# Fourier mixing and hash-routed experts in one kernel: idle products first, another order in the head, and row loads issued after the relus

## The chip, the core and the metric

The kernel runs on one core of one Trainium2 chip. The metric is the device time of one execution in microseconds (us); the figure compared is the median of several runs. Engines are named as in the profile: PE (TensorE, matrix products), DVE (VectorE), ACT (ScalarE), POOL (GpSimd) and SP (SyncE, which only issues DMAs here). ACT and POOL issue DMAs too. "Clock" is the TensorE clock that the throttle granted, 1.0 being full speed.

## What is computed

```python
X = np.fft.rfft(x, axis=1)                       # x: (8, 2496, 256), f32
Y = X * (filt_r + 1j * filt_i)[None, :, :]
y = np.fft.irfft(Y, n=2496, axis=1)              # (8, 2496, 256)
t = y.reshape(19968, 256)                        # one row per token
expert_idx = token_ids * np.int64(2654435761) % np.int64(8)
for e in range(8):                               # w1: (8, 256, 1024), w2: (8, 1024, 256)
    mask = expert_idx == e
    out[mask] = np.maximum(t[mask] @ w1[e], 0.0) @ w2[e]
```

A filter over the sequence of each batch, and then a two-layer network whose weights are chosen by a hash of the token's number. All of it is f32.

## The kernel before

*The filter.* A transform of 2496 points is split into 39 by 64. Stage 1 (`stage1`, for the first two batches `stage1_c`) multiplies x with the table `wf_t` into PSUM tiles `pa`; `forward` makes the products `pb` with the table `d_t`, and DVE applies the filter; `back` makes `pc` with the table `e_t`; `stage3` multiplies with `wi_t` (`pd`), and POOL scatters the resulting token rows (L380, L382, an indirect DMA for each group of rows) to their slots in the DRAM tensor `xs`. The slots are sorted by expert, so that 256 neighbouring rows, a tile, belong to one expert. `load1`, `load2` and `load4` are the loads ahead of the three stages (x, `mid<-d` and `t<-d` in the profile); between its stages a batch goes through DRAM (`d<-mid`, written by ACT's queue), except the first two, which stay in SBUF. The products run with a ring of four PSUM tiles `fps`, which ACT and DVE empty.

*The network.* There are up to 85 tiles of 256 rows; 80 are always used, and with these inputs no more than these. For a tile i, in `step(i)`:

- `weight_sums(i + 1)`: four subtractions of 128x512 on POOL (`tw`, L792) and `store(i - 1)`: two indirect DMAs on POOL to the output;
- `up(i)`: the first layer as seven products of half size (56 matmuls, `up_a`, `up_b`, `up_c`), summed by DVE (L809); ACT copies `h21` out of PSUM (L813) after the first of them and applies four relus (L806). Between that copy and the rest stands a hook, `between`, which calls `load(i + 2)`;
- `load(i)` (L750): four DMAs of 64 KB for a tile's rows (`xg<-xs`) and one for its rows' numbers (`no<-xs`), on ACT's queue (on SP's for tiles 0 and 1);
- `weights(i + 2, 0)` and, after `down`, `weights(i + 2, 1)`: 1 MB each on SP's queue, done only if the expert changes;
- `token_parts(i + 1)` (L773) transposes the next tile's rows on DVE, `token_sums(i + 1)` makes its four sums;
- `down(i)`: 32 products `dps` (L837) with the relus' results as their weights, and a copy `osb` on DVE (L842).

*What sets the order.* Nothing is scheduled by the compiler: every engine takes its instructions as the Python code emits them. The pieces of the filter are in a list `todo` with times. Those below zero are the head (`pre`), sorted by hand-written numbers from -160 to -75: tables and x of the second batch, stage 1, the middle (`chain`), stage 3 and the scatters of the first two batches, and meanwhile the routing (`count`, `route`, `places`). Those from zero on (`main`) are in units of tiles and are emitted inside `step`: up to i + .6 after `up`, up to i + .7, .8 and .9 after each quarter of `down`, the rest after it. `begin()` opens the pools of the tiles' loop and calls `load(0)` and `load(1)`. `put_off` holds the stores of batch 2's stage 1 that are not written at once (960, 600 and 40 KB). Tiles come in five stages: those of the first stage (0 to 9) hold tokens of the first two batches only, so the loop can start when these are scattered; the later stages end at tiles 20, 30, 50 and 80.

*Shared memory.* `wts` has four slots of 1 MB: the weights of two tiles. In the head slots 0 to 2 also hold the first batch's x and later its result, and slot 3 the second's first x and then the third's.

*Counters.* In the built program the DMAs of SP and ACT together use eight completion counters in turn, in the order in which the code emits them; a DMA waits until the one eight places before it has landed.

*The end.* After the loop come, outside any condition, the transposes of tiles 80 to 84 (L773, into `mid`) and the loads of tiles 82 to 84; then nested blocks run under `tc.If(used > ...)`, none of which is taken here.

Of the kernel before, what the change touches and what calls it, by code (L numbers as in the profile page):

```python
# [11 lines left out]
F32 = mybir.dt.float32  # L12
# [7 lines left out]
P = 128  # L20
# [16 lines left out]
NU = (HN + XG) // XG  # L37
# [6 lines left out]
NT = (N + E * (TB - 1)) // TB  # L44
# [8 lines left out]
NSURE = NT - 5  # L53
# [65 lines left out]
def kernel(  # L119
# [10 lines left out]
    nc = tc.nc  # L130
# [22 lines left out]
    banks = {k: pool(ctx, f"bank_{k}", 1, PSUM) for k in "abcd"}  # L153
# [241 lines left out]
    def weights(i, which):  # L395

        if i >= NT:
            return
        if i >= 2 and which == 0:
            ws[i] = ws[i - 2][0:2]  # L400
        eng, kw = nc.scalar if i < 2 else nc.sync, {}
        if which == 0:
            ws[i].append(eng.value_load(chunk_i[0:1, 0, i:i + 1], min_val=0, max_val=E - 1))
            if i >= 2:
                ws[i].append(eng.value_load(chunk_i[0:1, 1, i:i + 1], min_val=0, max_val=1))
        e = ws[i][2]
        if i >= 2:
            kw = {"cond": ws[i][3]}
        if which == 0:


            for f in (slice(0, F // 2), slice(F // 2, F)) if i < 2 else (slice(0, F),):
                eng.dma_start(out=ws[i][0][:, :, f],
                              in_=moe_w1[bass.ds(e, 1)].rearrange("one (p dp) f -> p (one dp) f", p=P)[:, :, f], **kw)
        else:
            eng.dma_start(out=ws[i][1], in_=moe_w2[bass.ds(e, 1)].rearrange("one (fp p) d -> p (one fp) d", p=P), **kw)
# [19 lines left out]
    def load_tables(part):  # L436
        if part < 2:

            nc.gpsimd.tensor_copy(junk[:], first.x[2 * part][0:1, 0, 0:1])
        sl = S_PARTS[part]  # L440
        nc.sync.dma_start(out=d_t[:, sl, :], in_=d_dram.ap()[:, sl, :])
        for k in range(2):
            load_filter(k, sl)
# [218 lines left out]
    def spaced(t0, t1, n):  # L662
        return [t0 + (t1 - t0) * u / n for u in range(n)]
# [10 lines left out]
    def part2(b, at, loads, lag):  # L674
        bt = batches[b]
        return (within([(at[u], lambda u=u: bt.forward(u)) for u in range(NS // 2)], .3) +
                within([(at[u] + lag, lambda u=u: bt.back(u)) for u in range(NS // 2)] +
                       [(loads[g], lambda g=g: bt.load2(g)) for g in range(NS // SG)]))

    def part3(b, at, loads):  # L680
        bt = batches[b]
        return within([(at[u], lambda u=u: bt.stage3(u)) for u in range(NU)] +
                      [(loads[v], lambda v=v: bt.load4(v)) for v in range(NV)])
# [10 lines left out]
                step(batches[j // (NS // 2)], j % (NS // 2))  # L694


    todo = [(t, lambda k=k: load_tables(k)) for k, t in enumerate((-160, -159, -157, -156))]
    todo += [(t, lambda v=v: second.load1(v)) for v, t in enumerate((-158, -156.5, -156.4))]
    todo += [(t, lambda u=u: first.stage1_c(u)) for u, t in enumerate(spaced(-155, -151, NU))]
    todo += [(-154.2, count), (-152, route), (-150.9, later)]  # L700
    todo += [(-137.2, places), (-128, tile_experts), (-121, experts), (-90, blanks)]
# [2 lines left out]
    todo += [(t, lambda k=k: way_back(k)) for k, t in enumerate((-150.44, -146.5, -141.8, -137.5, -133.8))]  # L704
    todo += [(-150.4, lambda: first.turn2(0))]
    todo += [(t, lambda k=k: chain(k)) for k, t in enumerate(spaced(-150, -105, NS + 2))]
    todo += [(t, lambda u=u: second.stage1_c(u)) for u, t in enumerate(spaced(-147.5, -132, NU))]
    for bt, at in ((first, spaced(-123.7, -105, NU)), (second, spaced(-103, -85, NU))):
        todo += [(t - 2.6, lambda bt=bt, u=u: bt.turn4(u)) for u, t in enumerate(at)]
        todo += [(t, lambda bt=bt, u=u: bt.stage3(u)) for u, t in enumerate(at)]  # L710
    todo += [(-135, lambda: nc.sync.dma_start(out=wi_t[:], in_=wi_dram.ap()))]
    todo += [(t, lambda v=v: batches[2].load1(v)) for v, t in enumerate((-119, -117.5, -116))]
    todo += [(t, lambda u=u: batches[2].stage1(u)) for u, t in enumerate((-101.5, -99.5, -84.8, -84.7, -84.6, -84.5))]

    todo += [(-75.5, lambda: [nc.scalar.dma_start(out=dram, in_=chip) for dram, chip in put_off])]
    todo += [(t, lambda k=k: weights(k // 2, k % 2)) for k, t in enumerate((-101, -98, -95, -92))]
    todo += [(-84.9, lambda: begin())]

    def batch(b, t1, t2, t3):
# [8 lines left out]

    todo += [(-75 + .1 * g, lambda g=g: batches[2].load2(g)) for g in range(4)]
    todo += [(-75.3 + .1 * v, lambda v=v: batches[3].load1(v)) for v in range(2)]  # L730
    todo += part2(2, spaced(.5, 3, N_2), [None] * 4 + [1], .6)
    todo += part3(2, spaced(4.3, 7.3, NU), [3.4, 3.6, 4.5]) + part1(3, spaced(1, 4, NU), [None, None, 2])
    todo += part2(3, spaced(6.4, 10, N_2), [5.2, 5.4, 5.6, 6.5, 7.5], .6)
    todo += part3(3, spaced(12, 16, NU), [11.2, 11.4, 12.5])
    todo += batch(4, (7.5, 11), (12.4, 16.4), (18.3, 22.3)) + batch(5, (13, 17), (18.4, 21.6), (23.2, 26.8))
# [3 lines left out]
    main = [t for t in todo if t[0] >= 0]  # L739


    gath = work = outs = nums = tpool = None
    xg, to_rows, parts, sums, rows = {}, {}, {}, {}, {}

    def begin():
        nonlocal gath, work, outs, nums, tpool
        rctx.close()
        gath, work, outs = pool(ctx, "gath", 2), pool(ctx, "work", 1), pool(ctx, "outs", 2)
        nums, tpool = pool(ctx, "nums", 8), pool(ctx, "tp", 2)
        for i in range(2):  # L750
            load(i)

    def load(i):

# [28 lines left out]
            nc.vector.tensor_tensor(st[:, k, :], p, q, op=op)  # L783
        parts[i]["sums"] = st

    def weight_sums(i, eng=None):

        eng, w1, h = eng or nc.gpsimd, ws[i][0], F // 2
        b11, b12, b21, b22 = [w1[:, d, f * h:f * h + h] for d in range(DP) for f in range(2)]
        t = [tpool.tile([P, h], F32, name=f"tw_{i}_{k}", tag=f"tw{k}") for k in range(4)]  # L790
        for k, (p, q) in enumerate(((b12, b11), (b22, t[0][:]), (b22, b12), (b21, t[1][:]))):
            eng.tensor_tensor(t[k][:], p, q, op=OP.subtract)  # L792
        sums[i] = t

    def up(i, ht, between=lambda: None):
        w1, x, st, t = ws[i][0], parts[i], parts[i]["sums"], sums[i]
        ps = {k: banks[k].tile([P, 4, P], F32, name=f"up_{i}_{k}", tag=k) for k in "abc"}
        h11, h12, h21, h22 = [ht[:, h, 4 * f:4 * f + 4, :] for h in range(2) for f in range(2)]

        def product(bank, w, xx, first, fs=range(4)):  # L800
            for f in fs:
                nc.tensor.matmul(out=ps[bank][:, f, :], lhsT=w[:, f * P:(f + 1) * P], rhs=xx,  # L802
                                 start=first and f == 0, stop=True, skip_group_check=True)

        def relu(out, in_):
            nc.scalar.activation(out=out, in_=in_, func=AF.Relu)  # L806

        def plus(out, bank, other):
            nc.vector.tensor_tensor(out, ps[bank][:], other, op=OP.add)  # L809

        h = F // 2
        product("a", w1[:, 0, 0:h], x[0, 0], True)
        nc.scalar.copy(out=h21, in_=ps["a"][:])  # L813
        between()
        product("b", t[1], st[:, 1, :], True)
        plus(h12, "b", h21)
        product("c", t[0], st[:, 0, :], True)
        plus(h22, "c", h21)
        product("a", w1[:, 1, 0:h], x[0, 1], False, (0, 1))
        product("b", t[2], st[:, 2, :], False)  # L820
        plus(h22, "b", h22)
        relu(h22, h22)
        product("a", w1[:, 1, 0:h], x[0, 1], False, (2, 3))
        relu(h11, ps["a"][:])
        product("c", w1[:, 1, h:], st[:, 3, :], False)
        plus(h12, "c", h12)
        relu(h12, h12)
        product("b", t[3], x[1, 1], False)
        plus(h21, "b", h21)
        relu(h21, h21)  # L830
# [23 lines left out]
        piece()  # L854
    token_parts(0)
    token_sums(0)
    weight_sums(0, nc.vector)
    used = []

    def run_until(t):  # L860
# [3 lines left out]
    def step(i):  # L864
        ht = work.tile([P, 2, FP, P], F32, name=f"ht_{i}", tag="ht")
        if i + 1 < NSURE:
            weight_sums(i + 1)
        if i > 0:
            store(i - 1)
        up(i, ht, lambda: load(i + 2) if i + 2 < NT else None)  # L870
        weights(i + 2, 0)
        if i + 1 < NSURE:
            token_parts(i + 1)
            token_sums(i + 1)
        run_until(i + .6)
        down(i, ht, lambda k: run_until(i + .7 + .1 * k) if k < 3 else None)
        weights(i + 2, 1)
        run_until(i + 1)
# [5 lines left out]
    assert not main  # L884
    store(NSURE - 1)

    for i in range(NSURE, NT):
        token_parts(i, mid[:, i - NSURE, 0:2 * TB].rearrange("p (d h t) -> p d h t", d=DP, h=2))
        if i + 2 < NT:
            load(i + 2)  # L890
    blocks = [range(NSURE, NSURE + 1), range(NSURE + 1, NSURE + 2), range(NSURE + 2, NT)]

    def rest(k):
        with tc.If(used[0] > blocks[k][0]):
            for i in blocks[k]:
                ht = work.tile([P, 2, FP, P], F32, name=f"ht_{i}", tag="ht")
                token_sums(i)
                weight_sums(i, nc.vector)
                up(i, ht)
                weights(i + 2, 0)  # L900
                down(i, ht)
                store(i)
                weights(i + 2, 1)
            if k + 1 < len(blocks):
                rest(k + 1)
# [29 lines left out]
```

## Time and profile before

| | |
|---|---|
| median of 9 runs | 1508.66 us (1504.43 to 1512.66) |
| the profiled execution | 1510.03 us, span 1508.2 us, mean clock 0.975 |
| PE busy | 1414.6 us, 94% of the span |
| DVE, ACT, POOL busy | 54%, 27%, 51% |
| first product, first product of tile 0 | 8.36 us, 160.55 us |
| last product | 1495.4 us |

The span has two parts: a head of some 160 us, in which the first two batches are filtered and scattered, and the loop over 80 tiles, which up to about tile 47 carries the other six batches along. The page's slices show the second, long part with PE at 90% or more, and slices with a lower granted clock in it:

```profile
PE   6987699899999979999989999999999999999996
```

In the quiet last third a stretch of 100 us looks like this (columns: sum of busy time of PE, weight load, DVE, ACT, POOL with their counts, then granted clock, DMA share, GB/s):

```profile
1300.00:1400.00 100.00, 100.00 (x672) 93.78 (x672) 58.01 (x87) 23.11 (x39) 50.21 (x43) 1.00 0.33 95
```

That is 7.6 tiles, 13.16 us each, with PE never idle. A stretch early in the loop, in which pieces of the filter stand between the tiles' products, shows both idle time and the halved clock:

```profile
260.50:267.40 6.90, 6.13 (x15) 4.77 (x16) 0.57 (x4) 2.34 (x5) 0.00 (x0) 0.51 0.40 98
```

An instruction's line in the answers below reads: start in us, duration, engine, line, operation, out<-in, shape, count, and in brackets the idle time of that engine before it with what ended it.

### The profile page before, as it was taken

How to read it: one execution, taken by the hardware profiler on the slowest of the kernel's cores; microseconds unless marked ns; L12 is line 12 of the kernel's file. 1: busy time of each engine (PE TensorE's matmuls, PEld its weight loads, DVE VectorE, ACT ScalarE, POOL GpSimd, SP SyncE). 2: the span in 40 equal slices, each digit the busy share in tenths (PEclk: the TensorE clock that was granted, in tenths of full speed). 3: DMA queues.
4: the chain of work that ended last, by engine and by line, in shares of the span. 5: the costliest groups of instructions: out<-in, count | busy, mean ns of one | idle time of the engine just before them, and what ended most of it. 6: DMA issues, size and time to landing. Idle time of an engine off the chain costs nothing.

```text
span 1508.2 us, 24354 instructions
## 1 busy us (share of the span) xinstructions
PE 1414.6 (94%) x8746; PEld 1285.9 (85%) x8746; DVE 812.9 (54%) x1374; ACT 401.8 (27%) x710; POOL 775.1 (51%) x700
## 2 busy tenths in 40 slices
PE   6987699899999979999989999999999999999996
PEld 6975588788978868888978999999999999999996
DVE  6862465266465546533654466634455555646563
ACT  3553032222223213322222222223222222221221
POOL 5056332663375455657524476467655546455551
PEclk9998799999999999999999999999999999999998
DMA  8236667746987597797753753556432424241412
GB/s 223 63 109 211 184 189 191 211 151 218 272 247 250 160 279 221 232 281 237 248 160 97 206 149 122 160 159 195 143 100 67 119 71 123 59 137 43 142 37 54
DMA packets 234105, 245.70 MB, mean 163 GB/s; under 512 B 128605, under 2 KB 206352, under 8 KB 226862
## 3 DMA queue, kind: packets, MB, share of 16 engines
q1 hardware_dynamic: 77079, 140.92, 30.4%
q10 hardware_dynamic: 136982, 58.59, 15.8%
q0 software_dynamic: 19920, 44.59, 8.6%
q8 instruction: 72, 1.18, 0.3%
q14 instruction: 52, 0.42, 0.1%
HBM read 251.19 MB, written 75.14 MB: 216 GB/s over the span
## 4 chain that ended last, share of the span: by engine, by line
PE 77%; DMA 7%; DVE 2%; issue 2%; another core or an unknown queue 1%; ACTq 1%; ACT 1%; SPq 0%; POOL 0%; DVEq 0%; POOLq 0%
PE dps L837 35%; PE up_b L802 13%; PE up_a L802 8%; PE up_c L802 8%; PE pb L269 3%; PE pc L292 3%; PE pa L225 3%; PE pd L225 3%; DMA xg<-xs 2%; DMA t<-d 2%; ACTq L762 1%; DMA mid<-d 1%; ACT ht L806 1%; DMA d<-mid 1%
## 5 line engine op out<-in xcount | busy, mean ns | idle before, releaser
L837 PE MATMUL dps<-wts,ht 128*128 128x256 f32 x2560 | 588.4, 383 | 20.3 <-ACT ht L806 20.3
L837 PEld LDWEIGHTS dps<-wts,ht 128*128 128x128 f32 x2560 | 487.0, 192 | 91.6 <-ACT ht L806 23.3
L792 POOL TENSOR_TENSOR tw<-wts 128x512 f32<-128x512 f32 x158 | 204.9, 1297 | 212.2 <-DMA wts<-in_moe_w_dram 178.0
L382 POOL DMA_INDIRECT xs<-o,sidx x176 | 175.3, 996 | 213.8 <-issue 90.1
L809 DVE TENSOR_TENSOR ht<-up_b,ht 128x512 f32<-128x512 f32 x240 | 165.8, 691 | 197.7 <-PE up_b L802 150.6
L847 POOL DMA_INDIRECT out_dram<-osb,no x160 | 158.5, 990 | 203.1 <-DVE osb L842 170.3
L806 ACT ACTIVATE ht<-ht 128x512 f32<-128x512 f32 x240 | 149.4, 629 | 346.1 <-DVE ht L809 151.1
L792 POOL TENSOR_TENSOR tw<-wts,tw 128x512 f32<-128x512 f32 x158 | 205.1, 1298 | 6.2
L802 PE MATMUL up_a<-xt,wts 128*128 128x128 f32 x1280 | 185.0, 278 | 16.9 <-DVE xt L773 11.7
L842 DVE COPY osb<-dps 128x512 f32<-128x512 f32 x80 | 55.3, 691 | 261.0 <-PE dps L837 215.6
L802 PEld LDWEIGHTS up_a<-xt,wts 128*128 128x128 f32 x1280 | 170.2, 194 | 22.6 <-issue 13.7
L802 PE MATMUL up_b<-st,tw 128*128 128x128 f32 x1280 | 172.8, 279 | 5.1 <-DVE ht L809 4.3
L802 PEld LDWEIGHTS up_b<-st,tw 128*128 128x128 f32 x1280 | 158.0, 194 | 7.7 <-POOL tw L792 3.8
L813 ACT COPY ht<-up_a 128x512 f32<-128x512 f32 x80 | 46.9, 586 | 370.4 <-PE up_a L802 347.3
L809 DVE TENSOR_TENSOR ht<-up_c,ht 128x512 f32<-128x512 f32 x160 | 110.4, 690 | 63.6 <-PE up_c L802 48.1
L279 DVE TENSOR_TENSOR z<-pb,filt 64x512 f32<-64x512 f32 x160 | 110.1, 688 | 37.6 <-PE pc L292 35.5
L783 DVE TENSOR_TENSOR st<-xt 128x128 f32<-128x128 f32 x160 | 97.8, 611 | 2.8
L802 PE MATMUL up_b<-xt,tw 128*128 128x128 f32 x640 | 85.0, 276 | 5.0 <-DVE ht L809 5.0
L275 DVE TENSOR_TENSOR y<-pb,filt 128x512 f32<-128x512 f32 x80 | 55.1, 689 | 63.8 <-PE pb L269 54.7
L802 PE MATMUL up_c<-st,wts 128*128 128x128 f32 x640 | 86.0, 278 | 0.4 <-issue 0.4
L802 PE MATMUL up_c<-st,tw 128*128 128x128 f32 x640 | 84.7, 275 | 0.0
L802 PEld LDWEIGHTS up_b<-xt,tw 128*128 128x128 f32 x640 | 77.9, 192 | 5.8 <-POOL tw L792 5.8
(142 smaller groups left out, 1330.5 us busy)
## 6 DMA issues: line engine op xcount, KB each, us to landing
wts<-in_moe_w_dram SPq DMA_DIRECT2D x160, 1024.0 KB
xg<-xs ACTq DMA_DIRECT2D x332, 64.0 KB
mid<-d SPq DMA_DIRECT2D x60, 256.0 KB
d<-mid ACTq DMA_DIRECT2D x60, 256.0 KB
d<-mid ACTq DMA_DIRECT2D x12, 960.0 KB
t<-d SPq DMA_DIRECT2D x12, 960.0 KB
x<-in_x_dram SPq DMA_DIRECT2D x36, 312.0 KB
x<-in_x_dram SPq DMA_DIRECT2D x21, 234.0 KB
```

Source lines behind the costliest of these rows:

```text
L225: nc.tensor.matmul(out=ps[0:cols * H, k, :], lhsT=w[:], rhs=src[:, 2 * i + k, :], start=True, stop=True)
L275: nc.vector.tensor_tensor(out=y[:], in0=ps[:], in1=f_t[0][:, sl, :], op=OP.mult)
L279: nc.vector.tensor_tensor(out=z[b], in0=ps[a], in1=f_t[1][64 * hi:64 * hi + 64, s1:s1 + 2, :], op=OP.mult)
L382: st = nc.gpsimd.indirect_dma_start(out=xs[:], out_offset=bass.IndirectOffsetOnAxis(ap=index, axis=0), in_=rows, in_offset=None, bounds_ch ...
L783: nc.vector.tensor_tensor(st[:, k, :], p, q, op=op)
L792: eng.tensor_tensor(t[k][:], p, q, op=OP.subtract)
L802: nc.tensor.matmul(out=ps[bank][:, f, :], lhsT=w[:, f * P:(f + 1) * P], rhs=xx, start=first and f == 0, stop=True, skip_group_check=True)
L806: nc.scalar.activation(out=out, in_=in_, func=AF.Relu)
L809: nc.vector.tensor_tensor(out, ps[bank][:], other, op=OP.add)
L837: nc.tensor.matmul(out=ps[:, h, :], lhsT=ht[:, h, fp, :], rhs=w2[:, fp, :], start=(fp == 0), stop=(fp == FP - 1))
L842: nc.vector.tensor_copy(out=rows[i][:], in_=ps[:])
L847: st = nc.gpsimd.indirect_dma_start(out=out[:], out_offset=bass.IndirectOffsetOnAxis(ap=to_rows[i][:, h:h + 1], axis=0), in_=o[:, h, :], i ...
```

## The change

Eight edits.

1. Fourteen products of the identity with itself, into PSUM bank a, are put first of all (time -165).
2. In the head, second's x[0] is asked for before the first part of the tables (-159.5 in place of -158). Its first two units of stage 1 are emitted together at -147.7 and -147.4, the others from -143 on.
3. The weights of tiles 0 and 1 are asked for at -110.2, -107 and -104, and tile 1's second half at -84.72 (before: -101, -98, -95, -92). All six units of batch 2's stage 1 now come after `begin()`, which is at -84.9; before, two of them stood at -101.5 and -99.5. Tile 1's second half of weights uses the slot that held batch 2's x[0], so it comes after these units.
4. `put_off` goes to SP's queue, behind the loads of tiles 0 and 1.
5. Three of the four subtractions `weight_sums(0)` on DVE are made in `begin()`, the fourth where all four stood.
6. `load(i + 2)` is called after `up(i)`, and so emitted after its four relus on ACT; the hook `between` is gone.
7. Batch 2's forwards and backs are given times by hand, one forward in tile 0 and three in each of tiles 1 to 3, and its stage 3 starts at 5.2 in place of 4.3, its loads later with it.
8. After the loop only the transposes of tiles 80 and 81 stay outside the condition; the loads and transposes of tiles 82 to 84 are inside it.

The test `len(ws[i]) == 2` in place of `which == 0` reads the expert's number in the same calls as before.

```diff
-    todo = [(t, lambda k=k: load_tables(k)) for k, t in enumerate((-160, -159, -157, -156))]
-    todo += [(t, lambda v=v: second.load1(v)) for v, t in enumerate((-158, -156.5, -156.4))]
+    def warm(n):
+        ps = banks["a"].tile([P, 4, P], F32, name="warm", tag="a")
+        for k in range(n):
+            nc.tensor.matmul(out=ps[:, k % 4, :], lhsT=ident[:], rhs=ident[:], start=True, stop=True)
+
+    todo = [(-165, lambda: warm(14))]
+    todo += [(t, lambda k=k: load_tables(k)) for k, t in enumerate((-160, -159, -157, -156))]
+    todo += [(t, lambda v=v: second.load1(v)) for v, t in enumerate((-159.5, -156.5, -156.4))]
...
-    todo += [(t, lambda u=u: second.stage1_c(u)) for u, t in enumerate(spaced(-147.5, -132, NU))]
+    todo += [(t, lambda u=u: second.stage1_c(u)) for u, t in enumerate([-147.7, -147.4] + spaced(-143, -132, NU - 2))]
...
-    todo += [(t, lambda u=u: batches[2].stage1(u)) for u, t in enumerate((-101.5, -99.5, -84.8, -84.7, -84.6, -84.5))]
-    todo += [(-75.5, lambda: [nc.scalar.dma_start(out=dram, in_=chip) for dram, chip in put_off])]
-    todo += [(t, lambda k=k: weights(k // 2, k % 2)) for k, t in enumerate((-101, -98, -95, -92))]
+    todo += [(t, lambda u=u: batches[2].stage1(u)) for u, t in enumerate((-84.8, -84.75, -84.7, -84.65, -84.6, -84.5))]
+    todo += [(-75.5, lambda: [nc.sync.dma_start(out=dram, in_=chip) for dram, chip in put_off])]
+    todo += [(t, lambda k=k: weights(k // 2, k % 2)) for k, t in enumerate((-110.2, -107, -104, -84.72))]
...
-    todo += part2(2, spaced(.5, 3, N_2), [None] * 4 + [1], .6)
-    todo += part3(2, spaced(4.3, 7.3, NU), [3.4, 3.6, 4.5]) + part1(3, spaced(1, 4, NU), [None, None, 2])
+    f2 = [.85] + [k + d for k in (1, 2, 3) for d in (.51, .53, .74)]
+    b2 = [1.5] + [k + d for k in (1, 2, 3) for d in (.72, .85, 1.5)]
+    todo += [(t, lambda u=u: batches[2].forward(u)) for u, t in enumerate(f2)]
+    todo += [(t, lambda u=u: batches[2].back(u)) for u, t in enumerate(b2)] + [(1.9, lambda: batches[2].load2(4))]
+    todo += part3(2, spaced(5.2, 7.8, NU), [4.5, 4.55, 5.2]) + part1(3, spaced(1, 4, NU), [None, None, 2])
...
         for i in range(2):
             load(i)
+        weight_sums(0, nc.vector, range(3))
...
         product("a", w1[:, 0, 0:h], x[0, 0], True)
         nc.scalar.copy(out=h21, in_=ps["a"][:])
-        between()
         product("b", t[1], st[:, 1, :], True)
...
-        up(i, ht, lambda: load(i + 2) if i + 2 < NT else None)
+        up(i, ht)
+        if i + 2 < NT:
+            load(i + 2)
         weights(i + 2, 0)
...
-    for i in range(NSURE, NT):
+    for i in range(NSURE, NSURE + 2):
         token_parts(i, mid[:, i - NSURE, 0:2 * TB].rearrange("p (d h t) -> p d h t", d=DP, h=2))
-        if i + 2 < NT:
-            load(i + 2)
...
                 ht = work.tile([P, 2, FP, P], F32, name=f"ht_{i}", tag="ht")
+                if i >= NSURE + 2:
+                    for j in ((i, i + 1) if i == NSURE + 2 else (i + 1,)):
+                        if j < NT:
+                            load(j)
+                    token_parts(i)
                 token_sums(i)
```

## The prediction

> **What bounds the kernel now.** I read the page first (busy shares, slices, the chain that ended last), then PE's waits by releaser, then PE's and ACT's timelines around the longest of them.
>
> ```profile
> PE 1414.6 (94%) x8746; PEld 1285.9 (85%) x8746; DVE 812.9 (54%) x1374; ACT 401.8 (27%) x710; POOL 775.1 (51%) x700
> PEclk9998799999999999999999999999999999999998
> PE 77%; DMA 7%; DVE 2%; issue 2%; another core or an unknown queue 1%; ACTq 1%; ACT 1%; SPq 0%; POOL 0%; DVEq 0%; POOLq 0%
> ```
>
> TensorE is busy for 94% of the span, and in quiet stretches without a gap. The diff removes none of its products, so only three things can be gained: PE's idle gaps (80.6 us, summed over its timeline; 37.5 of them before 162 us, where the tiles' loop begins), the half-clock stretches that follow a gap, and the ends of the span. After 162 us PE's waits are these:
>
> ```profile
> PE dps L837 <- ACT ht L806: 20.3, 8, 8.9
> PE up_b L802 <- DVE ht L809: 9.3, 11, 1.7
> PE up_a L802 <- ACT ht L813: 3.8, 3, 3.3
> PE pb L269 <- DMA mid<-d: 3.8, 1, 3.8
> ```
>
> The first line is half of it: eight times `down` waits for a relu. The longest, first on ACT, then on PE:
>
> ```profile
> 533.48 0.59 ACT L813 COPY ht<-up_a 128x512 f32<-128x512 f32 x1 [6.50 <-PE up_a L802]
> 533.81 7.41 ACTq L762 DMA_DIRECT2D xg<-xs  x4
> 546.24 0.38 ACTq L762 DMA_DIRECT2D no<-xs  x1
> 546.67 0.63 ACT L806 ACTIVATE ht<-ht 128x512 f32<-128x512 f32 x1 [12.61 <-DMA out_dram<-osb,no]
> 547.84 3.38 PE L837 MATMUL dps<-wts,ht 128*128 128x256 f32 x8 [8.88 <-ACT ht L806]
> 553.65 1.89 PE L837 MATMUL dps<-wts,ht 128*128 128x256 f32 x8
> ```
>
> Between the copy of h21 and the first relu ACT stands 12.6 us in the five issues of `load(i+2)`. In the built program the DMAs of SP and ACT take eight completion counters in turn, and each waits until the one eight places before it in the list has landed; so a row load of ACT is held by SP's 256-1024 KB loads ahead of it. Eight products then take 3.38 us where the next eight take 1.89.
>
> **Part 1: rows asked for behind the relus (every tile).** The same five DMAs per tile, on the same queue, are issued after the last relu, not after the first copy. `up` is 56 products of some 0.13 us, so about 7.5 us later. Gone is PE's wait, 20.3 us, and the cold products behind it: behind the 8.88 gap 3.38-1.89 = 1.5; behind the gaps at 261 and 790 us eight products take 3.78 (1.9 too much each) and the group of transform products after them some 1.2 and 0.9 too much. Together about 7.5, in all 28. It is given back where ACT still stands in the issue during `down`, whose pieces need ACT to empty PSUM (0.6 us copies at L222, L295, L227): the two longest blocks (533.50-546.62 and 779.71-789.46 us) less 7.5 leave 5.6 and 2.3, all others (7.1 at most) nothing beyond their own issue of 2.4 us, if what they wait for lands at the same moment. I take off 6: **-22**, bounds -30 (the L809 waits shrink too) and 0 (all reappears at a PSUM copy). The later landing is covered: issued at 7.8 to 10.1 us of a tile of 13.2 us and landing some 4 us later, rows are wanted by the transpose of L773 about 19.5 us after the tile's start. Without that cover (4 us) it would be a wait at DVE's transpose in each tile.
>
> **Part 2: the head, up to tile 0's first product at 160.55 us.**
>
> ```profile
> 8.36 6.87 PE L315 MATMUL pa<-wf_t,wts 117*128 117x120 f32 x32 [8.36 <-DMA wts<-in_x_dram]
> 31.15 3.10 PE L315 MATMUL pa<-wf_t,wts 117*128 117x120 f32 x16 [3.97 <-DMA wts<-in_x_dram]
> 37.33 1.94 PE L315 MATMUL pa<-wf_t,wts 117*128 117x120 f32 x16
> 116.29 0.99 POOL L382 DMA_INDIRECT xs<-o,sidx  x1 [2.62 <-ACT o L227]
> 128.33 4.75 ACTq L413 DMA_DIRECT2D wts<-in_moe_w_dram  x2
> 147.38 0.90 POOL L382 DMA_INDIRECT xs<-o,sidx  x1 [0.30 <-issue]
> 160.55 2.05 PE L802 MATMUL up_a<-xt,wts 128*128 128x128 f32 x8 [11.73 <-DVE xt L773]
> ```
>
> (a) Idle products and the order of x: 32 products take 6.87 us cold; at 16 in 1.94 they would take 3.9, so 14 idle ones before x save up to 3.0 in place. PE then waits for second's x, which landed at 31.15; asked for before the first part of the tables (0.77 MB, at the 223 GB/s of the page's first slice about 3.5 us) it lands near 27.6. The tables land no later than x did, and DVE starts its chain from both. -3, bounds -5 and +1.5 (the tables become the late ones).
> The granted clock reaches 1.00 at 14.8 us, 6.4 us after the first product. The Trainium skill ("TensorE: Matmul & The Clock Gate", section "Part 1: The HAM clock gate") says that the gate opens after a busy window of about 3.4 us of activity and advises against fitting a count of cold products. By that rule the idle products are worth at most half of 3.4, an estimate of 1.7 us, against 3.0 by the rows, and they help only if they run without a break into the first real ones.
>
> (b) Weights earlier, stage 1 of batch 2 later. Second's 22 scatters run from 116.29 to 147.38+0.9 = 32.0 us; a scatter with its issue is 1.29, so packed they take 28.5. The difference stands around the weights' issue at 128.33, which holds ACT for 4.75 us and o's copies with it, and around batch 2's stage 1 on PE. -3.5, bounds -5 and 0 (weights asked for at -110 now stand before the first batch's copies instead). The six units of stage 1, some 2 us each, fit in PE's wait of 11.7 before tile 0; without it they would cost 12.
>
> (c) The stores put off go from ACT to SP, behind the loads of tiles 0 and 1.
>
> ```profile
> 152.00 7.62 DMA xg<-xs
> 1503.20 2.02 DMA xg<-xs
> ```
>
> Both are row loads in the chain: the first shares the engines with 1.6 MB of stores issued at the same time, the second has them alone. -5.6, and 0.3 for the early weight sums (three of DVE's four 0.7 us subtractions, beside the last scatters): -5.9, bounds -7 and -3. Should the stores, now in the same queue as the rows and behind them, still share with tile 1's five DMAs, tile 0 is not touched by it.
>
> Sum of part 2: **-12.4**, bounds -17 and -1.5.
>
> **Part 3: a new wait in tile 0.** SP's loads of batch 3's x and of batch 2's d follow `load(2)` in the counters' turn. Before, `load(2)` was issued 2.1 us after tile 0 began, and mid<-d still came late:
>
> ```profile
> 175.04 1.87 PE L269 MATMUL pb<-mid,d_t 128*128 128x256 f32 x4 [3.81 <-DMA mid<-d]
> ```
>
> Now it goes out at 10.4, lands near 14, and the first mid<-d after it lands near 20 (5 us, as the chain has it), while the forward at .85 wants it 14 us after the tile's start. A stall of 6.5 and 2.5 cold, against 3.8 and 1.8: **+3.5**, bounds -5 (the stage is no longer late) and +6. What queues behind it is SP's weights(2).
>
> **Part 4: batch 2's forwards and backs, three per tile in place of four, stage 3 a tile later.** No work is added. The gaps it may end or make are of the size of the one at 299 us (3.3, L813, and as much cold) and of the small ones at 220 and 708 us (1.6, 1.7): **0**, bounds -4 and +4.
>
> **Part 5: the end.** Outside the condition stay two transposes; the row loads of tiles 82 to 84 (ACT, 1496.8 to 1504.2 us) go, 80 tiles being used.
>
> ```profile
> L930 POOLq DRAIN  x3: 46/103/5132, 1502.3 to 1508.0; - x3
> ```
>
> The chain ends with the last transpose (1506.06), but POOL's drain, which follows the landing of the last stores (1500.75), runs 5.13 us to 1507.38 by itself. **0**, bounds -5 (the drain too waits for the loads) and 0.
>
> The sum: 1510.0 (the profiled execution; its span is 1508.2) -22 -12.4 +3.5 = 1479.1. That execution is 1.4 above the median of 1508.66, so **1478**.
>
> **Rivals.**
> *The relu's wait only moves* (20%): ACT stands in the same issue, now at the start of `down`; h21's copy or a piece's PSUM copy waits instead. For it: in steps with pieces ACT copies for PE all through `down`. Against: by then most of what the loads waited for has landed, and relus are wanted at once while a PSUM bank has three others. Then only the head remains, and a few us of the main loop: 1510-12.4+3.5-1.4 = 1500, or 1495 with 5 of the 22.
> *More than the sum* (14%): the drain ends earlier (-5), and tile 0 doesn't stall (-3.5-3.8): 1478-12 = 1466.
> *Slower* (7%): as in tile 0, SP's loads (weights, t<-d, mid<-d, x) wait in turn for row loads issued 7.5 us later. For it: some 25 steps had a row load blocked for 4 us or more, so the two queues do hold each other. Against: most of those loads are asked for two or more us ahead and the row loads of earlier tiles have long landed. Priced as in tile 0 at about 5 a step: it eats the whole 31 from 7 such steps on (31/5 = 6.2); ten give 1478+50 = 1528, less if some overlap.
> *The head doesn't gain* (4%): POOL's 1.29 us scatters are the head's bound, and rows come when they come: 1478+9 = 1487, inside the range.
>
> **The numbers.** Forecast 55% with its own range 1468 to 1490. The range 1462 to 1499 takes in the larger gain and most of the first rival, and leaves out the slower one and the rest. What a measurement tells from no change is about 0.2%, 3 us: faster 89%, same 3%, slower 8%.
>
> **What would show it.** Right: `dps <- ACT ht L806` falls from 20.3 to a few us, up_a of tile 0 starts near 148, a `mid<-d` wait of 6 to 7 us near 162, the first x16 of second's stage 1 without its gap. Wrong: new waits of PE on ACT's copies (L222, L295, L813) or on DVE's transposes; waits on `wts` or `t<-d` in steps 1 to 25; POOL's scatters still ending at 148.

## The result, and the profile after

The changed kernel takes 1521.39 us (median of 10 runs, 1515.69 to 1525.07), the kernel before 1508.62 us (median of 31). The ratio is 1.0085, with a 95% interval of 1.0068 to 1.0103: 13 us slower, where 31 us less were forecast. The profiled execution took 1528.12 us, 7 us above its median; its span is 1526.3 us.

From the page of the changed kernel: busy time by engine, the clock by slices, and the group of `down`'s products (after the bar: busy us, mean ns of one, idle us just before them).

```profile
PE 1424.6 (93%) x8774; PEld 1292.2 (85%) x8774; DVE 821.3 (54%) x1371; ACT 406.3 (27%) x710; POOL 775.7 (51%) x700
PEclk9997899999999999999999999999999999999998
L849 PE MATMUL dps<-wts,ht 128*128 128x256 f32 x2560 | 585.6, 382 | 0.1
```

The wait that the edit was to remove is gone: `down` waited 20.3 us for the relus and now 0.1. Yet PE's waits from tile 0's first product on (line waited at, what for, us in total, times, longest) come to 52 us, against 43 before (both without tile 0's own). The largest:

```profile
PE up_b L815 <- DVE ht L822: 9.7, 8, 2.6
PE pb L269 <- issue: 8.8, 5, 3.6
PE up_a L815 <- issue: 8.5, 2, 7.8
PE pb L269 <- DMA mid<-d: 6.5, 1, 6.5
PE pc L292 <- DVE z L279: 3.9, 2, 2.5
PE pb L269 <- DVE z L279: 3.9, 2, 2.3
PE up_c L815 <- DVE ht L822: 3.3, 1, 3.3
PE pd L219 <- DVE z L279: 3.2, 2, 2.6
...
```

The wait has moved to the filter's pieces: all of PE's waits at `pa`, `pb`, `pc` and `pd` but those for DMAs come to 25.4 us, against 3.5 before (1.9 and 1.6, both at `pb`). On the second chip of the table below it is the same, 27.5 against 4.9. (The waits for L822 at the head of the list stood in the kernel before too, 9.3 us at L809; on the second chip they are 1.3 before and 1.4 after, so they come with the chip more than with the edit. The 8.5 at `up_a` is, but for 0.7 of it, the wait of tile 0, whose first product falls inside the window.)

Where the time went is best read between ACT's copies of h21 (L813, then L826), one per tile. Chips differ, so the table, made from the traces, has the first pair and four kernels profiled on another chip, one after the other. Times are us. A profile is a single execution: on the second chip that of the changed kernel was 10 us above its median and that of the kernel before 6 us below, so this pair lies 18 us apart where the medians and the ratio give 2 to 5.

| stretch | before | after | before, 2nd chip | after, 2nd chip | rows on SP, 2nd chip | best, 2nd chip |
|---|---|---|---|---|---|---|
| start to tile 0 | 162.6 | 166.1 | 155.7 | 154.5 | 157.1 | 147.5 |
| tiles 0 to 3 | 90.6 | 101.2 | 92.7 | 102.2 | 85.9 | 93.8 |
| 4 to 8 | 108.1 | 110.5 | 100.9 | 107.1 | 93.8 | 93.8 |
| 9 to 12 | 72.2 | 70.9 | 68.3 | 74.4 | 76.6 | 75.6 |
| 13 to 17 | 100.0 | 111.4 | 99.2 | 105.5 | 97.9 | 98.0 |
| 18 to 21 | 100.7 | 103.6 | 101.1 | 101.2 | 87.2 | 87.7 |
| 22 to 28 | 121.5 | 118.1 | 118.9 | 113.9 | 117.1 | 115.8 |
| 29 to 32 | 83.7 | 73.3 | 81.2 | 75.0 | 71.3 | 71.2 |
| 33 to 46 | 222.7 | 226.0 | 222.4 | 224.8 | 222.4 | 222.4 |
| 47 to PE's end | 433.3 | 433.3 | 433.3 | 433.3 | 433.3 | 433.3 |

The edit gains what it should around the block of tile 30 (10 and 6 us less in tiles 29 to 32) and nothing around the larger one of tile 18. Tiles 0 to 3, 4 to 8 and 13 to 17 together lose more than that (24 and 22 us), and tile 0 starts 3.5 us later on the first chip and 1.2 us sooner on the second.

### The profile page after: what moved, and what is told of

It reads as the page before. It is cut to its first block, busy times and chain, and to the rows that moved or that the text cites. A ratio compares the mean times of both kernels' runs of the same rounds, so it can differ in the third digit from the quotient of the medians.

```text
span 1526.3 us, 24354 instructions
## 1 busy us (share of the span) xinstructions
PE 1424.6 (93%) x8774; PEld 1292.2 (85%) x8774; DVE 821.3 (54%) x1371; ACT 406.3 (27%) x710; POOL 775.7 (51%) x700
## 5 line engine op out<-in xcount | busy, mean ns | idle before, releaser
L382 POOL DMA_INDIRECT xs<-o,sidx x176 | 175.6, 998 | 219.0 <-ACT o L227 110.2
L822 DVE TENSOR_TENSOR ht<-up_b,ht 128x512 f32<-128x512 f32 x240 | 166.0, 692 | 198.4 <-PE up_b L815 148.4
L815 PE MATMUL up_a<-xt,wts 128*128 128x128 f32 x1280 | 183.9, 277 | 10.2 <-issue 8.5
L822 DVE TENSOR_TENSOR ht<-up_c,ht 128x512 f32<-128x512 f32 x160 | 110.4, 690 | 68.4 <-PE up_c L815 43.8
L826 ACT COPY ht<-up_a 128x512 f32<-128x512 f32 x80 | 46.9, 587 | 350.4 <-PE up_a L815 300.9
L225 PE MATMUL pd<-t,wi_t 120*117 120x256 f32 x320 | 83.2, 405 | 14.2 <-DVE t L355 10.5
```

The costliest lines, as they stand in the source:

```text
L225: nc.tensor.matmul(out=ps[0:cols * H, k, :], lhsT=w[:], rhs=src[:, 2 * i + k, :], start=True, stop=True)
L382: st = nc.gpsimd.indirect_dma_start(out=xs[:], out_offset=bass.IndirectOffsetOnAxis(ap=index, axis=0), in_=rows, in_offset=None, bounds_ch ...
```

## The experiments

Ratios are to the kernel before, run beside them on the same chip, with 95% intervals.

### Each part alone

```diff
only_load, to the kernel before:
-        up(i, ht, lambda: load(i + 2) if i + 2 < NT else None)
+        up(i, ht)
+        if i + 2 < NT:
+            load(i + 2)
```

> The kernel before with edit 6 alone: load(i+2) is issued behind the relus. Prediction's own theory: about -22 us (ratio 0.985). Theory LATE (rows issued late hold SP's loads and ACT's copies in down, so the wait only moves and more): +3 to +12 us (1.002 to 1.008), with the wait of down for the relus gone but waits on DVE's z, ACT's copies and on mid<-d in its place. Rival BATCH2 (the new places of batch 2's forwards cost it): -5 to -15 us here.

`only_batch2` has edit 7 alone, `only_head` edits 1 to 5, `only_tail` edit 8.

> The kernel before with edit 7 alone: batch 2's forwards, backs and stage 3 at their new places. Prediction: 0 (-4 to +4). Rival BATCH2: +8 to +13 us, with PE waiting at the second of two adjoining forwards in tiles 1 to 3, 2 to 4 us each. Theory LATE: within 4 us of before.

> The kernel before with edits 1 to 5 alone. Prediction: -12.4 us, tile 0 starting at 148 us. From the profile after, where tile 0 starts at 164.0 in place of 160.6 us: +3 us. If the head's edits carry the whole loss it would be +12 us.

> The kernel before with edit 8 alone: loads and transposes of tiles 82 to 84 inside the condition. Prediction: 0 (POOL's drain ends last anyway), bounds -5 and 0. If the drain waits for nothing of the row loads, the span from PE's last product to the end stays at 12.8 us; if the chain of row loads sets the end it falls by up to 5.

| | median us | ratio | interval |
|---|---|---|---|
| only_load | 1515.11 | 1.0006 | 0.9979 to 1.0033 |
| only_batch2 | 1509.33 | 0.9983 | 0.9963 to 1.0003 |
| only_head | 1515.44 | 1.0033 | 1.0008 to 1.0059 |
| only_tail | 1512.36 | 1.0002 | 0.9974 to 1.0030 |

(The kernel before: 1513.34.) Rows behind the relus bring nothing by themselves: the -22 is missing, and my guess of +3 to +12 was too dark as well. The largest of PE's waits from tile 0 on in `only_load`:

```profile
PE up_b L802 <- DVE ht L809: 10.0, 11, 2.4
PE pb L269 <- DMA mid<-d: 8.2, 1, 8.2
PE up_c L802 <- DVE ht L809: 5.1, 2, 4.0
PE pb L269 <- DVE z L279: 4.7, 3, 1.6
PE pb L269 <- issue: 4.4, 4, 2.4
```

The 20.3 us at the relus are gone from the list, and the waits at the filter's pieces, without those for DMAs, have grown from 3.5 to 20.3 us. So the wait moves with this edit alone.

The head costs 5 us by the ratio (1 to 9 by its interval, 2 by the medians) where -12.4 was forecast. (Within the change, `all_again` against `not_head` below, it costs nothing; why more alone was not settled.) Batch 2's new places cost nothing alone, so as a cause by themselves they fall, and the end is worth nothing. Added up the four make +4 us, not +13.

### Each part left out

```diff
not_load, to the changed kernel:
         nc.scalar.copy(out=h21, in_=ps["a"][:])
+        between()
...
-        up(i, ht)
-        if i + 2 < NT:
-            load(i + 2)
+        up(i, ht, lambda: load(i + 2) if i + 2 < NT else None)
```

> The changed kernel once more, as the yardstick of this chip. Expected: the ratio found before, 1.0085 (1.007 to 1.010), some +13 us. If the four parts just add up (head +5, load +1, batch 2 -3, end 0) it would be +3 us (1.002).

> The changed kernel with load(i+2) put back between h21's copy and the rest of up (edit 6 undone). Theory LATE: the loss of the whole falls by 5 us or more (ratio to before 1.000 to 1.005) since batch 2's new places were bad only together with late rows. Rival (parts add up): +2 us from before, so no nearer to before than the whole by more than 2 us.

> The changed kernel with batch 2's pieces at their old places (edit 7 undone). If batch 2's places and the late rows only hurt together, this too falls to +2 to +6 us. If the parts add up it is 3 us slower than the whole.

> The changed kernel with the head as before (edits 1 to 5 undone). If the head costs what it costs alone (+5), this is 5 us nearer to before than the whole, at +8 us (1.005); if the head's only loss was that tile 0 starts 3.5 us later, +10 us.

| | median us | ratio | interval |
|---|---|---|---|
| all_again (the changed kernel) | 1521.48 | 1.0057 | 1.0036 to 1.0078 |
| not_load | 1513.98 | 1.0002 | 0.9979 to 1.0025 |
| not_batch2 | 1518.21 | 1.0038 | 1.0011 to 1.0065 |
| not_head | 1523.14 | 1.0062 | 1.0034 to 1.0089 |

(Before: 1512.81.) With the row loads back at their old place the whole loss is gone. Where the rows stay late so does the loss, whatever else is undone; without batch 2's places it may be some 3 us less, which the intervals don't separate. (Rows late with nothing else changed, `only_load`, cost nothing, so it takes more than that edit.) Single profiles show late rows and batch 2's new places at work together. From ACT's h21 copy of tile 0 to that of tile 9 it takes 199 to 205 us with neither (before, only_head, only_tail), 199 and 206 with the rows late alone (only_load, not_batch2), 195 and 201 with batch 2's new places alone (only_batch2, not_load), and 210 to 217 with both (after, all_again, not_head). Most of the difference are three waits of PE at the second of two adjoining `pb`, in tiles 1 to 3: 2.23, 2.28 and 3.64 us in the profile after, within 0.02 us the same in the other profiles with both (all_again, not_head and, on the second chip, after_third), and not there with batch 2's new places alone, which have one wait of 2.0 or 3.1 us for an ACT copy.

What happens there can be seen in tile 1 of the changed kernel. ACT's timeline (start, us, engine, line, operation; in brackets the idle time before):

```profile
196.20 0.63 ACT L819 ACTIVATE ht<-ht 128x512 f32<-128x512 f32 x1 [0.26 <-DVE ht L822]
196.27 1.82 ACTq L774 DMA_DIRECT2D xg<-xs  x4
198.12 0.95 ACTq L774 DMA_DIRECT2D no<-xs  x1
199.12 0.59 ACT L295 COPY mid<-pc 128x512 f32<-128x512 f32 x1 [2.28 <-PE pb L269]
```

and PE's:

```profile
195.28 1.03 PE L292 MATMUL pc<-y,e_t 128*128 128x256 f32 x4
196.14 1.89 PE L225 MATMUL pa<-x,wf_t 117*120 117x256 f32 x8
197.87 1.03 PE L269 MATMUL pb<-mid,d_t 128*128 128x256 f32 x4
201.13 1.10 PE L269 MATMUL pb<-mid,d_t 128*128 128x256 f32 x4 [2.23 <-issue]
```

PE has filled its four PSUM tiles (`pc`, two `pa`, `pb`) while ACT issues five DMAs, none of them held up (2.8 us in all). ACT begins to empty the first only at 199.12 and is through at 199.71, 0.8 us after PE stopped. The second `pb` doesn't take that tile: by the built program it takes the tile of the first `pb`, and in the trace it starts 0.10 us after DVE's last read of that (201.03). In `only_batch2`, with the loads at their old place, ACT copies `pc` at 192.62, before PE comes to the pair at 193.76, and the two run without a gap (eight `pb` products in 1.89 us). So the issue, which I had booked as hidden, stands ahead of the copies that the pieces wait for. Of the 2.2 us some 0.8 are that delay itself; the rest comes from the tile that the built program chose, and that it chose so because of the issue's new place is likely but was not tested apart from it.

Tile 20 of the changed kernel shows another cost, between POOL and DVE. POOL's timeline:

```profile
613.32 1.28 POOL L806 TENSOR_TENSOR tw<-wts 128x512 f32<-128x512 f32 x1 [2.92 <-DMA wts<-in_moe_w_dram]
614.68 1.27 POOL L806 TENSOR_TENSOR tw<-wts,tw 128x512 f32<-128x512 f32 x1
615.90 1.32 POOL L806 TENSOR_TENSOR tw<-wts 128x512 f32<-128x512 f32 x1
617.18 1.32 POOL L806 TENSOR_TENSOR tw<-wts,tw 128x512 f32<-128x512 f32 x1
```

and DVE's:

```profile
614.73 1.37 DVE L795 TENSOR_TENSOR st<-xt 128x128 f32<-128x128 f32 x1
616.13 1.24 DVE L795 TENSOR_TENSOR st<-st,xt 128x128 f32<-128x128 f32 x1
617.29 1.36 DVE L795 TENSOR_TENSOR st<-xt 128x128 f32<-128x128 f32 x1
618.57 0.28 DVE L795 TENSOR_TENSOR st<-xt,st 128x128 f32<-128x128 f32 x1
```

While POOL makes its weight sums, each of DVE's token sums takes as long as one of POOL's subtractions, 1.24 to 1.37 us, and 0.28 once POOL is through; the four take 4.3 us, 3 more than without POOL, and behind them PE waits 2.5 and 1.8 us for z, the filter's products on DVE. In the kernel before, whose loop comes to tile 20 after the block of tile 18, only the first of the four met POOL (0.92 us). The Trainium skill says as much ("SBUF — State Buffer", section "SBUF: two separate sides"): a DVE operation with two SBUF inputs and a GpSimd operation that reads SBUF take turns at one pair of ports, each for its whole length. The rows agree. That the edit brought the two together is read from this one pair of profiles.

### ACT out of the issue

```diff
rows_on_sp, to the kernel before; after_rows_on_sp, to the changed kernel:
-            ld = (nc.sync if i < 2 else nc.scalar).dma_start(out=to, in_=src)
+            ld = nc.sync.dma_start(out=to, in_=src)
after_rows_behind_down, to the changed kernel:
         up(i, ht)
-        if i + 2 < NT:
-            load(i + 2)
...
         down(i, ht, lambda k: run_until(i + .7 + .1 * k) if k < 3 else None)
+        if i + 2 < NT:
+            load(i + 2)
         weights(i + 2, 1)
```

> The kernel before, with the five row loads of a tile on SP's queue in place of ACT's, at the same place of the list (so the same counters, and no ACT standing in their issue). Theory ISSUE (what costs is ACT standing in the issue, 2.4 us and more, before the relus or before the pieces' copies): the wait of down for the relus falls from some 20 us to under 5 and nothing takes its place, -15 to -25 us (0.983 to 0.990). Rival SUPPLY (heavy tiles are bound by loads on SP and by DMA, whichever engine waits): within 5 us of before, with the waits at mid<-d, t<-d or wts.

> The changed kernel with the row loads on SP's queue, behind up as it has them. ISSUE: the waits of pb, pc and pd on fps behind the relus (tiles 1 to 3, 7, 14, 20, 21: 2 to 3.6 us each) vanish, -15 us or more against the changed kernel, below before (0.995 or less). SUPPLY: as the changed kernel, +8 to +13 us.

> The changed kernel with load(i+2) issued on ACT behind down(i) in place of behind up(i): neither the relus nor the first copies of the pieces stand behind it. ISSUE: -8 to -15 us against the changed kernel (ratio to before 0.995 to 1.001); what stays is that h21's copy of the next tile may stand behind it. SUPPLY (rows and the SP loads after them come later still): slower than the changed kernel, with waits at the transposes and at mid<-d.

| | median us | ratio | interval |
|---|---|---|---|
| rows_on_sp | 1451.86 | 0.9734 | 0.9706 to 0.9762 |
| after_rows_on_sp | 1453.39 | 0.9743 | 0.9711 to 0.9774 |
| after_rows_behind_down | 1492.99 | 1.0037 | 1.0011 to 1.0063 |

(Before, on this chip: 1490.48.) One word, the queue, takes 39 us off, more than was expected; the order of the list and the counters are the kernel before's. (On the second chip, `rows_sp_again` against `before_again`, PE's waits behind tile 0's first product are 12 us in place of 35, and its products take 10 us less, at a mean granted clock of 0.984 in place of 0.979.) All of PE's waits behind tile 0's first product, in `rows_on_sp`:

```profile
PE pd L225 <- DMA t<-d: 8.9, 2, 6.4
PE up_b L802 <- DVE tw L792: 1.1, 1, 1.1
PE up_a L802 <- ACT ht L813: 0.9, 2, 0.5
PE pd L225 <- ACT o L227: 0.7, 1, 0.7
PE up_b L802 <- DVE ht L809: 0.5, 1, 0.5
```

The relus' wait is gone and nothing but `t<-d` stands in its place. In `after_rows_on_sp` the three waits of tiles 1 to 3 are gone as well, and its time is that of `rows_on_sp`, so the place in the list no longer matters once ACT doesn't issue. That settles it: neither DMA nor the loads on SP bound these tiles; ACT standing in an issue did. (That the rows land sooner on SP's queue is not the reason: behind tile 0 PE waits for no transpose of rows, with either queue.) Each of the three places in ACT's order that were tried is one where somebody waits for ACT. Behind `down` the same issue stands in front of the next tile's h21 copy:

```profile
PE up_a L815 <- ACT ht L826: 25.8, 15, 6.3
```

15 waits, 25.8 us: more than the 20.3 that the edit was made against. So `after_rows_behind_down` misses the 0.995 to 1.001 that I expected; its 1.0037 is no better than the changed kernel's 1.0034 on the second chip. `rows_sp_again`, on the next chip, checks the gain:

> The kernel before with the row loads on SP's queue. If the gain is the queue's: 0.970 to 0.980 again on this chip. If it was that chip's: 0.985 to 1.000.

It took 1455.56 us, ratio 0.9770 (0.9743 to 0.9796): the gain holds.

### The head

```diff
after_w11_late, to the changed kernel:
-    todo += [(t, lambda k=k: weights(k // 2, k % 2)) for k, t in enumerate((-110.2, -107, -104, -84.72))]
+    todo += [(t, lambda k=k: weights(k // 2, k % 2)) for k, t in enumerate((-110.2, -107, -104, -75.4))]
```

> The changed kernel with the 1 MB second half of tile 1's weights asked for behind the loads of tiles 0 and 1 in place of just ahead of them. If it took the engines from tile 0's rows in the place of the stores put off, rows are at the transpose 4 to 5 us after their issue (9 to 10 in the changed kernel) and tile 0 starts 4 to 6 us sooner; the time falls by as much, 1.002 to 1.005 to before. Rival (the rows are slow by themselves or for another DMA): no change.

> The kernel before, profiled on the chip of this call. Ratio 1.000 (0.997 to 1.003). If late completions of PE come with the chip, its profile has them exactly if those of the three other kernels of this call do; tile 0 at 157 to 165 us with them, at 155 to 158 us without.

> The changed kernel. With late completions on this chip: +9 to +13 us and tile 0 as late as before's (within 3 us). Without: tile 0 starts 5 to 9 us sooner than before's, and the time is nearer to before's, 0 to +6 us.

`after_w11_late`: 1487.83 us, ratio 0.9989 (0.9962 to 1.0016). `before_again`: 1493.61 us, 1.0008 (0.9986 to 1.0030). `after_third`: 1495.35 us, 1.0034 (1.0014 to 1.0055). On that chip tile 0 starts at 153.57 us before and 152.41 us after, a gain of 1.2 where I had expected 5 to 9. Timelines of `after_third`: ACT's issue of tile 1's weights, POOL's last scatter, and SP's first row load:

```profile
131.04 0.43 ACTq L416 DMA_DIRECT2D wts<-in_moe_w_dram  x1
137.78 0.90 POOL L382 DMA_INDIRECT xs<-o,sidx  x1 [0.30 <-issue]
146.39 1.81 SPq L774 DMA_DIRECT2D xg<-xs  x4
```

and of `after_w11_late`:

```profile
137.84 0.43 ACTq L416 DMA_DIRECT2D wts<-in_moe_w_dram  x1
136.60 0.89 POOL L382 DMA_INDIRECT xs<-o,sidx  x1 [0.30 <-issue]
140.21 1.81 SPq L774 DMA_DIRECT2D xg<-xs  x4
```

The last scatter starts at 137.78 us in the one and 136.60 in the other, sooner than before (141.73 on the first's chip), as forecast. The rows wait for it to land: 8.6 us from its start, 3.6 us with the megabyte of weights issued behind it. Edit 4 takes 1.6 MB of stores off the engines at that moment and edit 3 puts 1 MB there.

The other profiles agree, and what counts in them is whether such a megabyte, weights or stores, is issued in the last 7 us ahead of the last scatter or behind it. In the ten profiles in which it is behind, the first row load follows the scatter's start by 2.3 to 3.6 us: 2.3 in the first profile before, whose stores are issued at 149.66, 2.3 us after the scatter; 2.7 in the first after; 3.6 in `after_w11_late` and `best`. In the ten in which it is ahead, by 6.0 to 9.4 us: 7.6 in `before_again`, whose stores are issued from 137.41 on; 8.6 in `after_third`; and 6.0 in `best2`, whose late weights were issued at 136.31, only 0.11 us ahead of its last scatter. So a late place in the list helps only where it comes out behind the scatter in time.

With the weights late, tile 0 starts at 146.24 us. That is not the forecast's 148 come true: the forecast started from 160.55, and on these chips the head of the kernel before starts tile 0 at 153.57 to 155.79 us (before_again, rows_sp_again, rows_on_sp). Chip by chip, in single profiles, the whole head with late weights gains 8.1 to 9.6 us and not 12.4 (145.45 in `best` against 153.57 and 154.98; 146.24 against 155.79), and the later weights alone 3 to 7 us (146.24 against 149.00 and 149.52; 145.45 against 152.41).

### What is late next

`best` joins rows on SP (old place, old batch 2), edits 1 to 5 and 8, and the late weights. `best2` has these lines more, and `best3` takes edit 4 back (the stores on ACT's queue).

```diff
best2, to best:
-    todo += [(-75.3 + .1 * v, lambda v=v: batches[3].load1(v)) for v in range(2)]
+    todo += [(-74.5 + .1 * v, lambda v=v: batches[3].load1(v)) for v in range(2)]
...
-    todo += part3(3, spaced(12, 16, NU), [11.2, 11.4, 12.5])
+    todo += part3(3, spaced(12, 16, NU), [10.4, 10.6, 12.5])
```

> Row loads on SP's queue at their old place in up, with the changed kernel's head (edits 1 to 5), its end (edit 8) and tile 1's second half of weights behind the first row loads; batch 2's pieces at their old places. Adding up: rows_sp_again less 5 to 9 us where the head's gain shows, less 0 to 2 us where it doesn't.

> best with batch 2's loads (mid<-d) asked for ahead of batch 3's x in place of behind it, and batch 3's first two loads of t<-d asked for 0.8 of a tile sooner. If the head's gain was only held up there: the waits at mid<-d (8.1) and t<-d (5.6) fall to 0 to 5 together, -7 to -12 us against best (0.969 to 0.972). If mid<-d is held by the landing of the stores put off: mid<-d still waits 4 us or more, -3 to -7 us.

> best2 with edit 4 undone: the stores put off are issued on ACT's queue, ahead of the rows' landing. If mid<-d was held by those stores: its wait goes, but tile 0's rows share the engines with 1.6 MB again and tile 0 starts 3 to 6 us later than in best2; in all within 3 us of best2. If edit 4 is worth what was forecast for it (5.6 us), best3 is 3 to 6 us slower than best2.

| | median us | ratio | interval |
|---|---|---|---|
| best | 1453.77 | 0.9765 | 0.9738 to 0.9791 |
| best2 | 1446.11 | 0.9696 | 0.9669 to 0.9724 |
| best3 | 1442.09 | 0.9674 | 0.9646 to 0.9702 |

`best` starts tile 0 9.5 us sooner than `rows_sp_again`, on the same chip, and takes only 2 us less. Its largest wait:

```profile
PE pb L269 <- DMA mid<-d: 8.1, 1, 8.1
```

Batch 2's way through DRAM doesn't get sooner with tile 0, so PE waits for it there instead. Asked for ahead of batch 3's x it comes nearly in time: in `best2` the waits there are 2.6 us. (Its ratio is 0.0069 below that of `best`, but the two ran on different chips, on which the kernel with the rows on SP alone has 0.9734 and 0.9770; half of the step can be the chips'.) `best3` is no slower than `best2` (the intervals overlap), and tile 0 starts at 148.67 us in the one and 148.45 in the other, so edit 4 isn't worth its 5.6 us: that step of the forecast isn't borne out. `best3`'s waits from tile 0's first product on, that product's own first:

```profile
PE up_a L812 <- DVE xt L782: 14.6, 1, 14.6
PE pb L269 <- DMA mid<-d: 2.9, 1, 2.9
PE dps L847 <- DMA wts<-in_moe_w_dram: 1.9, 1, 1.9
PE up_a L812 <- ACT ht L823: 1.3, 2, 0.9
PE up_b L812 <- DVE ht L819: 0.5, 1, 0.5
```

## Why the prediction was wrong

*Part 1 (-22; measured: nothing alone, and 7.5 us dearer within the change, `all_again` against `not_load`).* The wait was read rightly and its removal too: 20.3 us went to 0.1. The step that failed is that the other blocks leave "nothing beyond their own issue of 2.4 us": I took the issue to cost nothing behind the last relu. The rows of tile 1 show that PE pays for the issue itself, not only for a blocked one, and the lists of waits show how much: what left the relus (20.3 us) came back at the filter's pieces (3.5 us before, 20.3 in `only_load`, 25.4 after). `rows_on_sp` shows that it is ACT's standing in the issue, since without it 39 us go. (A slip besides: 5.6 and 2.3 are 7.9, and I took off 6, so the term should have read -20.) This was my first rival ("the relu's wait only moves", 20%), and its mechanism, a piece's PSUM copy that waits instead, is what the rows of tile 1 show; its price of 1495 to 1500 was too low, because I let it only cancel the gain, and because it gave the head its full -12.4. Two adjoining forwards (part 4) are nearly harmless with ACT free (one wait of 2.0 us in `only_batch2`) and cost 2.2 to 3.6 us in each of tiles 1 to 3 with ACT in an issue; each part was priced against the other parts as they had been.

*Part 2 (-12.4; measured -1.2 on one chip, +3.5 in the first pair).* (a) The idle products did their work in place: 32 products took 3.80 us after, 6.87 before, so they saved 3.1, the 3.0 by the rows and not the lower 1.7, although PE stood idle for 2.2 us between them and the first real product. (In that profile the clock then fell to 0.51 from 15 to 18 us and half of it was lost again: the next 56 products took 8.04 us, 6.42 in `after_third`.) On the second chip the first batch's stage 1 then ended 2 us sooner and second's x[0] was there 5 us sooner, but x[1], which had kept its place, now made PE wait 3.7 us at 38 us, and the first scatter started at 78.44 us against 78.09. A bound that I gave (the tables late) had the right form and the wrong operand. (b) Right: on the second chip the second batch's scatters took 27.2 us from the first's start to the last's in place of 31.5 (forecast: -3.5; measured 110.61 to 137.78 and 110.26 to 141.73, that is -4.3). (c) Failed: the stores went and the weights came, +2.8 us between the last scatter and tile 0 on the second chip and +0.7 in the first pair, in place of -5.9. The prediction priced the stores' leaving and not the arrival of the megabyte of weights that edit 3 moves to that moment.

*Part 3 (a stall of 6.5 us).* Right in kind: 6.48 us in the first profile after, 7.8 and 10.2 in the two other profiles of this kernel. That the first falls on the 6.5 forecast is luck.

*Parts 4 and 5.* Right alone: 0.9983 and 1.0002. The end between PE's last product and the end of the span went from 12.8 to 12.0 us though the row loads are gone, so they did not set it; that POOL's drain does fits, but no run leaves it out.

*The slower rival* (7%) was SP held by late row loads. Its mark, `mid<-d` late in tile 0, is there and was booked; elsewhere it hardly is: PE's other waits for loads in the loop come to 0.2 us in the first profile after and 5.6 in `after_third`, and with rows and all loads on one queue (`rows_on_sp`) to 8.9. So the change was slower for a reason that I had as "no gain". The forecast's error was less in any one price than in booking every gain in full and, of the places where the moved work would stand, only those in which it had stood before.

## What to carry to other kernels

DMAs issued by an engine that also computes are work of that engine: here five issues are 2.4 us in its order, and 4 to 13 us when one of them waits. Moving them within ACT's order exchanged one waiting reader for another; moving them to the queue of SP, which computes nothing here, removed the wait. Before a wait is booked as gone, look for who waits at the new place; and when a stretch that starts sooner is forecast, name every operand of its next steps with its own arrival: what kept its place is what is waited for next.

## What the runs showed of the hardware that was not expected

Chips differ. The kernel before took 1508 to 1513 us in three series and 1490 to 1492 us in three others. In the slower ones what waits for PE sometimes starts 1 to 6 us after the modelled end of its products. In the head of the profile after, PE's transposes of a unit end at 133.6 us (131.72 and 1.91), and DVE's copy of them starts at:

```profile
139.34 1.42 DVE L355 COPY t<-pu 120x512 f32<-120x512 f32 x2 [9.76 <-remote]
```

In `after_third` a unit's transposes start at 120.21 us and take 1.04, and the copy starts at:

```profile
120.85 1.29 DVE L355 COPY t<-pu 120x512 f32<-120x512 f32 x2 [1.90 <-PE pu L351]
```

The copy waits for PE alone in the built program; the profile, which names PE as what it waited for in `after_third`, names an unknown source (`remote`) in the other. It starts 0.64 us after the first of PE's transposes in the one, while they still run, and 5.7 us after the last in the other. It came in all ten profiles of those chips, in before as in after, in each of them in the head and around tile 26 and in most around tiles 6 and 13, and in none of the ten on the other chips. What it is stays open. That it made the changed kernel's loss larger (1.0085 and 1.0057 there, 1.0034 on the one chip without it) is possible but was not shown apart, and the intervals of the last two overlap.
